# One expert's second weight matrix loaded whole, and the expert outputs joined in one piece

## The chip, the core and the metric

The kernel runs on one core of one Trainium2 chip. The metric is the time of one execution on the device in microseconds (us); for the kernel before, the median of three runs is 180.59 us (180.25 to 180.80). A profile of one execution, taken by the hardware profiler, goes with it. Its times count from the start of its span.

The engines are named as in the profile: PE multiplies matrices (PEld is its loading of weights), DVE and ACT work on vectors, POOL here does nothing but issue transfers, SP issues one. Transfers (DMA) are carried out by sixteen DMA engines.

## The reference

Attention over 8 batches of 8 heads with 576 positions and 64 columns a head, with a sliding window (four heads) or a dilated window (four heads), gives `x` of 4608 rows and 512 columns. A soft mixture of 8 experts, with 4 slots each, follows:

```python
logits = x @ phi                                  # 4608 x 32
d = softmax of logits over the rows
slot_input = d.T @ x                              # 32 x 512: 8 experts x 4 slots
for e in range(8):
    h = np.maximum(slot_input[e] @ w1[e], 0.0)    # w1[e]: 512 x 1024
    slot_out[e] = h @ w2[e]                       # w2[e]: 1024 x 512
c = softmax of logits over the 32 slots
return c @ slot_out                               # 4608 x 512, fp32
```

`w1` and `w2` of an expert have 2 MB each in fp32. They are turned to fp16 on their way into the core's memory, where each takes 1 MB.

## The kernel before, in words

**The main part** (lines 447 to 552) goes through the eight batches in a software pipeline whose order is written out by hand (`ORDER`, `STEPS`). It loads q, k and v of a batch, computes attention, the exponentials of the logits (`ET`, kept for all batches) and adds each batch's share to `U`, the sum that `slot_input` is made of. All inputs, w1 and w2 are loaded by transfers that POOL issues (`load_raw`, `load_w1`, `load_w2`), in one order for the whole kernel. POOL's transfers take turns on eight semaphores, so each issue waits until the transfer eight places ahead of it has landed.

**The order of the weights.** w1 of all experts and w2 of experts 0 to 2 are loaded between and behind the inputs. Once the last batch has left the raw buffers, line 538 gives their place to w2 of experts 3 to 7 and issues these loads (lines 545 to 549): experts 3 and 4 whole, one transfer of 1 MB each, then the left 256 columns of experts 5, 6 and 7, then their right 256 columns. A column half is two transfers of 256 KB (`load_w2` with `s`, line 208: four of the eight row blocks each).

**The experts** (lines 565 to 615). `rs` are the row sums of the softmax over the slots. `U` is divided by its last column into `si` (64 partitions: 32 slots of plain heads, 32 of dilated ones; 256 columns). `si` is turned over on PE in four transposes, two into each of two PSUM tiles `siT0` and `siT1`, and DVE copies the one and ACT the other into `siTm`, where each expert's slots stand in columns of their own. `hps` is the product with w1, `h_sb` its positive part, `hT` the transposed, `hTm` a copy of that (lines 593 to 615).

**The expert outputs** (`emit_so`, line 623). `so` is one PSUM tile of 128 partitions x 512 columns, to which all experts add. `emit_so(None, experts)` multiplies whole rows of w2 (512 columns), `emit_so(0, ...)` the left 256 columns, `emit_so(1, ...)` the right ones. The result lies in four partial sums on four groups of 32 partitions. They are joined in two steps, each for one half of 256 columns. `gather_so` copies `so` into `so_part` in fp16, 128 columns by DVE and 128 by ACT. `spread_so` multiplies with the constant `spread`, which adds the four groups up and puts the sum on all four (PSUM tile `rep`, 128 columns), and copies it into `so_sb`, again DVE for 128 columns and ACT for 128.

**The output** (`emit_fin`, line 654, and `emit_batch`, line 673). For 128 rows of the output, `f` is the product of `ET` with `so_sb`, and ACT and DVE in turn scale it with `rrow` into `om` (fp16). Four such blocks are a batch; POOL then issues the batch's store (line 676), whose transfer turns fp16 to fp32. `om[b]` lies where w1 of expert b was. The first six batches (`NHALF`) are stored in two halves of columns, the last two whole; the last 64 rows of each batch go out at the end from `om_l` (line 703).

**The order around the change** (lines 681 to 705). Every engine takes its instructions in the order of the program text, which is this:

```python
emit_so(None, (0, 1, 2, 3)); emit_so(None, (4,))
emit_so(0, (5,)); emit_so(0, (6,)); emit_so(0, (7,))
gather_so(0); spread_so(0)
for b in range(NHALF):
    if b in (2, 3, 5):
        emit_so(1, ({2: 5, 3: 6, 5: 7}[b],))
    if b == 5:
        gather_so(1)
    emit_batch(b, 0, DH)
spread_so(1)
for b in range(NHALF):
    emit_batch(b, DH, DMODEL)
```

So the left half of the columns is computed, joined and multiplied for six batches while the right halves of experts 5, 6 and 7 are still on their way; the right copy into `so_part` stands ahead of the sixth left batch, the right product and the copy into `so_sb` behind it.

Of the kernel before, what the change touches and what calls it, by code (L numbers as in the profile page):

```python
# [9 lines left out]
FP32 = mybir.dt.float32  # L10
FP16 = mybir.dt.float16
# [14 lines left out]
E_EXP = 8  # L26
S_PER_E = 4
N_SLOTS = 32
# [12 lines left out]
DH = DMODEL // 2  # L41
# [55 lines left out]
def kernel(  # L97
# [10 lines left out]
    nc = tc.nc  # L108
# [9 lines left out]
    ident = cst[:, o : o + 128]  # L118
    spread = cst[:, o + 128 : o + 256]
# [43 lines left out]
    ring = ctx.enter_context(tc.tile_pool(name="ring", bufs=2, space=bass.MemoryType.PSUM))  # L163
# [36 lines left out]
    def load_w2(e, s=None):  # L200
        src = moe_w2[e].rearrange("(p c) n -> p c n", p=128)
        if s is None:
            nc.gpsimd.dma_start(
                out=w2t[e].rearrange("p c n -> p (c n)"), in_=src.rearrange("p c n -> p (c n)")
            )
            return
        cols = slice(DH * s, DH * s + DH)
        for u in range(2):
            nc.gpsimd.dma_start(out=w2t[e][:, 4 * u : 4 * u + 4, cols], in_=src[:, 4 * u : 4 * u + 4, cols])  # L209
# [249 lines left out]
    for which in "QK":  # L459
        load_raw(which, 1)  # L460
    nc.gpsimd.dma_start(
        out=phi_raw.rearrange("p (u c) s -> p u (c s)", u=2),
        in_=moe_phi.rearrange("(u p c) s -> p u (c s)", u=2, c=2),
# [15 lines left out]
    def step(op, b):  # L479
        if op[0] in "ARM" and op[1:] in TILES:  # L480
            kind, i = TILES[op[1:]]
            if op[0] == "A":
                tmp[(op[1:], b)] = emit_av(b, kind, i)
            elif op[0] == "R":
                tmp[("R" + op[1:], b)] = emit_recip(b, kind, i, tmp[(op[1:], b)])
            else:
                engine = nc.scalar if op[1:] in ON_ACT else nc.vector
                norm_mult(b, kind, i, tmp.pop((op[1:], b)), tmp.pop(("R" + op[1:], b)), engine)
        elif op in ("S0", "S1", "S2"):
            tmp[(op, b)] = emit_scores(b, int(op[1]))  # L490
        elif op in ("E0", "E1", "E2"):
            emit_exp(b, int(op[1]), tmp.pop(("S" + op[1], b)))
        elif op in ("MK0", "MK1", "MK2"):
            emit_mask(b, int(op[2]))
        elif op[0:2] in ("QT", "KT", "VT"):
            turn(op[0], b, int(op[2]))
        elif op in ("XP0", "XP1"):
            tmp[(op, b)] = xT_plain(b, int(op[2]))
        elif op in ("XD0", "XD1"):
            tmp[(op, b)] = xT_dil(b, int(op[2]))  # L500
        elif op in ("XPc0", "XPc1", "XDc0", "XDc1"):
            xT_copy(b, op[1], int(op[3]), tmp.pop((op[0:2] + op[3], b)))
        elif op in ("VA", "VB", "VC", "VD"):
            tmp[(op, b)] = v_rows(b, "ABCD".index(op[1]))
        elif op in ("VAc", "VBc", "VCc", "VDc"):
            v_place(b, "ABCD".index(op[1]), tmp.pop((op[0:2], b)))
        elif op in ("LG", "EP"):
            tmp[(op, b)] = (back_logits if op == "LG" else back_erow)(b)
        elif op == "ET":
            back_et(b, tmp.pop(("LG", b)))  # L510
        elif op == "ER":
            back_er(b, tmp.pop(("EP", b)))
        else:
            {"ED": back_erd, "U": back_u, "UT": back_add}[op](b)

    def loads(which, b):
        load_raw(which, b)
        if which == "V":
            if b > 2:
                load_weights(1)  # L520
            if b == B - 1:
                load_weights(len(weights))
# [6 lines left out]
    for it in range(B + max(s for _, s in STEPS)):  # L529
        for op, stage in STEPS:  # L530
            b = it - stage
            if not 0 <= b < B:
                continue
            step(op, b)
            if op in frees and b + 2 < B:
                loads(frees[op], b + 2)
            left.discard((op, b))
            if w2b_pool is None and not left:
                raw_pool.release()
                w2b_pool = tc.alloc_tile_pool(name="w2b", bufs=1, side="right")  # L540
                for e in (3, 4, 5):
                    w2t[e] = w2b_pool.tile([128, 8, DMODEL], FP16, name=f"w2_{e}", tag=f"w2_{e}")
                slab_weights(6, "qk0", QK_SLAB)
                slab_weights(7, "qk1", QK_SLAB)
                for e in (3, 4):
                    load_w2(e)
                for s in range(2):
                    for e in (5, 6, 7):
                        load_w2(e, s)
        if it == 0:  # L550
            nc.vector.tensor_copy(
                out=phi4, in_=phi_raw[:, :, None, :].broadcast_to([128, 4, 4, N_SLOTS])
            )
# [21 lines left out]
        )  # L575
    nc.vector.reciprocal(out=rcol, in_=U[:, 4 * D : 4 * D + 1])
    nc.vector.tensor_scalar(out=si, in0=U[:, 0 : 4 * D], scalar1=rcol, scalar2=None, op0=ALU.mult)
    for k, copy in enumerate((nc.vector.tensor_copy, nc.scalar.copy)):
        siT = ring.tile([128, 2, N_SLOTS], FP16, name=f"siT{k}", tag="ring")
        rows = slice(32 * k, 32 * k + 32)  # L580
        for c in range(2):
            nc.tensor.transpose(siT[:, c, :], si[rows, 128 * c : 128 * c + 128], ident[rows, rows])
        diag = bass.AP(
            siTm.tensor,
            siTm.offset + 2 * k * E_EXP * N_SLOTS,
            [siTm.ap[0], (E_EXP * N_SLOTS, 2), (N_SLOTS + S_PER_E, E_EXP), (1, S_PER_E)],
        )
        copy(out=diag, in_=siT.rearrange("p c (e s) -> p c e s", e=E_EXP))
    nc.vector.reciprocal(out=rrow, in_=rs)
    hps = psum_e.tile([128, 2, 512], FP32, name="hps", tag="hps")  # L590
    h_sb = h_pool.tile([128, FDIM], FP16, name="h_sb", tag="h_sb")
# [1 line left out]
    for fc in range(2):  # L593
        for g in range(2):
            for dc in range(4):
                for j in range(4):
                    e = 4 * g + j
# [4 lines left out]
                        start=(g == 0 and dc == 0),  # L602
                        stop=(g == 1 and dc == 3),
# [3 lines left out]
    for c in range(8):  # L607
# [3 lines left out]
        out=hTm[:, 0].rearrange("p c (j s) -> p c j s", j=4)[:, :, :, 0:16], in_=hT4[:, :, :, 0:16]  # L611
    )
    nc.scalar.copy(
        out=hTm[:, 1].rearrange("p c (j s) -> p c j s", j=4)[:, :, :, 16:32], in_=hT4[:, :, :, 16:32]
# [6 lines left out]
    so = psum_so.tile([128, DMODEL], FP32, name="so", tag="so")  # L621

    def emit_so(s, experts):
        cols = slice(0, DMODEL) if s is None else slice(DH * s, DH * s + DH)
        for c in range(8):
            for e in experts:
                g, j = divmod(e, 4)
                row = 32 * (j if len(experts) == 4 else c % 4)
                nc.tensor.matmul(
                    so[row : row + 32, cols],  # L630
                    hTm[:, g, c, 32 * j : 32 * j + 32],
                    w2t[e][:, c, cols],
                    start=(e < 4 and c == 0),
                    stop=(e == 7 and c > 3),
                    skip_group_check=True,
                )

    def part_cols(s):
        c0 = DH * s
        return (nc.vector.tensor_copy, c0), (nc.scalar.copy, c0 + DH // 2)  # L640

    def gather_so(s):
        for copy, c0 in part_cols(s):
            copy(out=so_part[:, c0 : c0 + DH // 2], in_=so[:, c0 : c0 + DH // 2])

    def spread_so(s):
        for copy, c0 in part_cols(s):
            rep = ring.tile([128, DH // 2], FP32, name=f"rep_{c0}", tag="ring")
            nc.tensor.matmul(rep, spread, so_part[:, c0 : c0 + DH // 2], start=True, stop=True)
            copy(out=so_sb[:, c0 : c0 + DH // 2], in_=rep)  # L650

    turn = [0]

# [26 lines left out]

    NHALF = 6
    emit_so(None, (0, 1, 2, 3))
    emit_so(None, (4,))
    for e in (5, 6, 7):
        emit_so(0, (e,))
    gather_so(0)
    spread_so(0)
    for b in range(NHALF):
        if b in (2, 3, 5):
            emit_so(1, ({2: 5, 3: 6, 5: 7}[b],))  # L690
        if b == 5:
            gather_so(1)
        emit_batch(b, 0, DH)
    spread_so(1)
    for b in range(NHALF):
        emit_batch(b, DH, DMODEL)
    for b in range(NHALF, B):
# [4 lines left out]
    for e in range(2):  # L702
        nc.gpsimd.dma_start(
            out=rest[:, e, 512:576, :].rearrange("n i d -> i n d"), in_=om_l[64 * e : 64 * e + 64]
# [37 lines left out]
```

## Time and profile before

| | us |
|---|---|
| median of three runs | 180.59 (180.25 to 180.80) |
| the profiled execution's own time | 180.63 |
| its span, first to last instruction | 178.80 |
| busy PE, DVE, ACT, POOL in the span | 126.7, 126.3, 124.0, 56.2 |
| last whole w2 (expert 4) landed | 137.19 |
| last left piece landed, last right piece landed | 145.21, 153.24 |
| first f begins | 146.81 |
| first store issued, last store issued | 148.76, 167.67 |
| first store landed, last store landed | 154.60, 177.27 |

Transfers of POOL by kind, with the median time from issue to landing: whole weights 1 MB, 22.1 us; weight pieces of 256 KB, 15.8 us; half-width stores 512 KB, 6.2 us; whole-width stores 1 MB, 8.7 us. These times hold the wait in the queue behind earlier transfers, so they aren't the time that a transfer takes; that is read from the steps between landings.

A store or load counts as landed when all sixteen DMA engines have added their increment to its semaphore. The granted clock of PE is 0.853 in the mean, and 0.50 from 146.6 us to the end.

A row of the timeline reads: start, duration, engine, line, operation, output <- inputs, form and how many; in brackets the idle time of the engine just before, and what ended it. A row of the chain that ended last: start, duration, and what the chain stood on.

### The profile page before, as it was taken

What the parts mean: (1) busy time and instruction counts of PE and PEld (TensorE: products, weight loads), DVE (VectorE), ACT (ScalarE), POOL (GpSimd) and SP (SyncE); (2) the same over time, 40 slices, a digit from 0 to 9 for tenths busy, and PEclk for the clock granted to TensorE, in tenths of its full rate; (3) what the DMA queues carried; (4) which work ended last, traced back from release to release, by engine and by line L of the source; (5) the groups of instructions that cost most, each with busy time, mean ns of one, the idle gap of its engine ahead of it and who ended that gap; (6) DMA issues with size and microseconds to landing.
All of it is one profiled execution on the core that took longest, in us unless ns stands there. A gap on an engine that the chain in (4) does not pass through costs nothing.

```text
span 178.8 us, 4810 instructions
## 1 busy us (share of the span) xinstructions
PE 126.7 (71%) x2016; PEld 81.9 (46%) x2016; DVE 126.3 (71%) x277; ACT 124.0 (69%) x268; POOL 56.2 (31%) x94
## 2 busy tenths in 40 slices
PE   0015938988899998888988988986686856688000
PEld 0014625776666676567667657665332422221000
DVE  6464899999999999999999898275211016789200
ACT  6006758999999999999999989996301116688000
POOL 7544244224224224225420005111111515375400
PEclk9999999999999879999999699699957685555555
DMA  5999999999999999999999999999999999999994
GB/s 98 195 208 211 211 213 211 212 213 215 215 213 213 213 213 214 213 211 218 210 213 214 214 215 221 215 218 218 209 211 194 196 197 234 390 321 393 406 413 125
DMA packets 21445, 40.85 MB, mean 229 GB/s; under 512 B 1712, under 2 KB 14128, under 8 KB 20784
## 3 DMA queue, kind: packets, MB, share of 16 engines
q0 software_dynamic: 21280, 40.41, 114.3%
q8 instruction: 16, 0.26, 0.5%
q1 hardware_dynamic: 144, 0.14, 0.3%
q14 instruction: 5, 0.04, 0.1%
HBM read 62.07 MB, written 9.44 MB: 400 GB/s over the span
## 4 chain that ended last, share of the span: by engine, by line
DMA 56%; DVE 25%; PE 5%; issue 4%; ACT 3%; POOL 1%; POOLq 0%; DVEq 0%
DMA w<-in_moe_w_dram 36%; DMA rawK<-in_k_dram 9%; DVE qk L220 8%; DMA rawV<-in_v_dram 5%; DMA phi_raw<-in_moe_phi_dram 5%; DVE vT L220 5%; DVE p L282 5%; PE f L656 3%; ACT om L665 2%; DVE xd L330 2%; DVE om_l L669 1%; DVE xp L330 1%; POOL rawQ L189 1%; PE s L262 1%; DVE rc_P L317 1%
## 5 line engine op out<-in xcount | busy, mean ns | idle before, releaser
L271 ACT ACTIVATE p<-s 128x1920 f16<-128x1920 f32 (+1 forms) x24 | 42.7, 1779 | 10.9 <-PE s L262 10.8
L262 PE MATMUL s<-qk 32*128 32x128 f16 (+2 forms) x704 | 26.7, 295 | 17.9 <-DVE qk L220 12.6
L305 PEld LDWEIGHTS <-p 128*128 128x128 f16 (+1 forms) x480 | 23.0, 105 | 14.7 <-DVE xp L330 5.2
L242 ACT COPY vX<-rv 128x768 f16<-128x768 f16 (+1 forms) x32 | 25.9, 866 | 1.7 <-PE rv L236 1.7
L262 PEld LDWEIGHTS <-qk 32*128 32x128 f16 x704 | 17.2, 117 | 21.1 <-DVE qk L220 12.6
L326 ACT ACTIVATE xp<-o_P,rc_P 128x64 f16<-128x64 f32 x96 | 24.3, 406 | 2.7 <-DVE rc_P L317 2.7
L282 DVE TENSOR_TENSOR p<-p,masks 128x1920 f16<-128x1920 f16 (+1 forms) x24 | 25.4, 1083 | 0.0
L236 PE MATMUL rv<-cst,vT 128*128 128x128 f16 x176 | 18.7, 252 | 3.5 <-DVE vT L220 1.8
L220 DVE STREAM_TRANSPOSE qk<-rawQ 128x576 uint32<-128x576 uint32 x16 | 18.8, 1242 | 2.7 <-DMA rawQ<-in_q_dram 2.7
L305 PE MATMUL o_P<-vX,p 128*128 128x65 f16 (+1 forms) x288 | 20.0, 205 | 0.8 <-DVE xd L330 0.2
L220 DVE STREAM_TRANSPOSE qk<-rawK 128x576 uint32<-128x576 uint32 x16 | 19.5, 1231 | 1.1 <-DMA rawK<-in_k_dram 1.1
L220 DVE STREAM_TRANSPOSE vT<-rawV 128x576 uint32<-128x576 uint32 x16 | 19.5, 1226 | 0.7 <-DMA rawV<-in_v_dram 0.4
L236 PEld LDWEIGHTS <-vT 128*128 128x128 f16 x176 | 13.8, 128 | 8.2 <-issue 3.7
L209 POOL DMA_DIRECT2D w<-in_moe_w_dram x12 | 8.9, 746 | 26.7 <-DMA w<-in_moe_w_dram 18.7
L669 DVE TENSOR_SCALAR om<-f,rrow 128x256 f16<-128x256 f32 (+1 forms) x28 | 13.5, 519 | 4.1 <-PE f L656 3.4
L189 POOL DMA_DIRECT2D rawQ<-in_q_dram x16 | 8.9, 560 | 21.0 <-DVE rc_P L317 16.0
L665 ACT ACTIVATE om<-f,rrow 128x256 f16<-128x256 f32 (+1 forms) x28 | 12.8, 502 | 3.5 <-PE f L656 2.8
L656 PE MATMUL f<-so_sb,ET 32*128 32x256 f16 (+1 forms) x60 | 12.1, 420 | 3.7 <-ACT om L665 2.5
L676 POOL DMA_DIRECT2D out_dram<-om x14 | 10.4, 745 | 12.4 <-DVE om L669 9.4
L189 POOL DMA_DIRECT2D rawK<-in_k_dram x16 | 8.8, 551 | 17.4 <-DVE rc_P L317 15.0
L305 PE MATMUL o_D<-vX,p 128*128 128x65 f16 x128 | 10.1, 206 | 3.3 <-DVE xp L330 2.8
L189 POOL DMA_DIRECT2D rawV<-in_v_dram x16 | 8.7, 548 | 11.3 <-DVE rc_P L317 8.5
(83 smaller groups left out, 194.3 us busy)
## 6 DMA issues: line engine op xcount, KB each, us to landing
w<-in_moe_w_dram POOLq DMA_DIRECT2D x13, 1024.0 KB, 22.1
out_dram<-om POOLq DMA_DIRECT2D x12, 512.0 KB, 6.2
rawQ<-in_q_dram POOLq DMA_DIRECT2D x16, 288.0 KB, 10.8
rawK<-in_k_dram POOLq DMA_DIRECT2D x16, 288.0 KB, 10.1
rawV<-in_v_dram POOLq DMA_DIRECT2D x16, 288.0 KB, 9.8
w<-in_moe_w_dram POOLq DMA_DIRECT2D x12, 256.0 KB, 15.8
out_dram<-om POOLq DMA_DIRECT2D x2, 1024.0 KB, 8.7
out_dram<-om_l POOLq DMA_DIRECT2D x2, 512.0 KB, 9.3
```

Of the source, the lines that this page charges most:

```text
L189: nc.gpsimd.dma_start(out=t[g::2, :], in_=src[4 * g : 4 * g + 4].rearrange("h (p j) d -> (h p) (j d)", j=PJ),)
L220: nc.vector.transpose(out=out_, in_=in_)
L236: nc.tensor.transpose(rg[:, n_t, :, c, :], rows, ident)
L242: copy(out=vX[b % 2][:, t0 : t0 + n, :, 0:D], in_=rg.rearrange("p n h c d -> p n h (c d)"))
L262: nc.tensor.matmul(sps[:, h, c0 : c0 + w], kk, qq, start=(tt == 0), stop=(tt == 1))
L271: return nc.scalar.activation(out=pt, in_=sps[:, :, 0:n], func=AF.Exp, scale=SCALE)
L282: return nc.vector.tensor_tensor(out=pt, in0=pt, in1=m, op=ALU.mult)
L305: nc.tensor.matmul(o[rows, h, :], lhs, rhs, start=(n == 0), stop=(n == len(jobs) - 1), skip_group_check=True,)
L326: nc.scalar.activation(out=dst[:, h], in_=src[:, h], func=AF.Copy, scale=rc[:, h : h + 1])
L656: nc.tensor.matmul(fp[:, 0 : c1 - c0], ET[32 * j : 32 * j + 32, m : m + 128], so_sb[32 * j : 32 * j + 32, c0:c1], start=True, stop=True,)
L665: nc.scalar.activation(out=dst, in_=fp[:, 0 : c1 - c0], func=AF.Copy, scale=rrow[:, blk : blk + 1])
L669: nc.vector.tensor_scalar(out=dst, in0=fp[:, 0 : c1 - c0], scalar1=rrow[:, blk : blk + 1], scalar2=None, op0=ALU.mult)
```

## The change

w2 of expert 5 is loaded whole, behind experts 3 and 4; only experts 6 and 7 are loaded in column halves. Expert 5 is multiplied over all 512 columns ahead of the left halves, so nothing of it stands between the output batches any more. `gather_so` and `spread_so` become `join_so`: one copy of 256 columns by DVE, one product of 256 columns, one copy by ACT. The right join as a whole stands ahead of the sixth left batch. And `si` is turned over in two transposes of all 64 partitions into one PSUM tile, from which DVE and ACT copy their parts.

```diff
-                for e in (3, 4):
+                for e in (3, 4, 5):
                     load_w2(e)
                 for s in range(2):
-                    for e in (5, 6, 7):
+                    for e in (6, 7):
                         load_w2(e, s)
...
+    siT = ring.tile([128, 2, 2, N_SLOTS], FP16, name="siT", tag="ring")
+    for c in range(2):
+        nc.tensor.transpose(
+            siT[:, c].rearrange("p k s -> p (k s)"), si[:, 128 * c : 128 * c + 128], ident[0:64, 0:64]
+        )
     for k, copy in enumerate((nc.vector.tensor_copy, nc.scalar.copy)):
-        siT = ring.tile([128, 2, N_SLOTS], FP16, name=f"siT{k}", tag="ring")
-        rows = slice(32 * k, 32 * k + 32)
-        for c in range(2):
-            nc.tensor.transpose(siT[:, c, :], si[rows, 128 * c : 128 * c + 128], ident[rows, rows])
...
-        copy(out=diag, in_=siT.rearrange("p c (e s) -> p c e s", e=E_EXP))
+        copy(out=diag, in_=siT[:, :, k, :].rearrange("p c (e s) -> p c e s", e=E_EXP))
...
-    def gather_so(s):
-        for copy, c0 in part_cols(s):
-            copy(out=so_part[:, c0 : c0 + DH // 2], in_=so[:, c0 : c0 + DH // 2])
-
-    def spread_so(s):
-        for copy, c0 in part_cols(s):
-            rep = ring.tile([128, DH // 2], FP32, name=f"rep_{c0}", tag="ring")
-            nc.tensor.matmul(rep, spread, so_part[:, c0 : c0 + DH // 2], start=True, stop=True)
-            copy(out=so_sb[:, c0 : c0 + DH // 2], in_=rep)
+    def join_so(s):
+        cols = slice(DH * s, DH * s + DH)
+        nc.vector.tensor_copy(out=so_part[:, cols], in_=so[:, cols])
+        rep = ring.tile([128, DH], FP32, name=f"rep_{s}", tag="ring")
+        nc.tensor.matmul(rep, spread, so_part[:, cols], start=True, stop=True)
+        nc.scalar.copy(out=so_sb[:, cols], in_=rep)
...
-    emit_so(None, (4,))
-    for e in (5, 6, 7):
+    for e in (4, 5):
+        emit_so(None, (e,))
+    for e in (6, 7):
         emit_so(0, (e,))
-    gather_so(0)
-    spread_so(0)
+    join_so(0)
     for b in range(NHALF):
-        if b in (2, 3, 5):
-            emit_so(1, ({2: 5, 3: 6, 5: 7}[b],))
+        if b in (3, 5):
+            emit_so(1, ({3: 6, 5: 7}[b],))
         if b == 5:
-            gather_so(1)
+            join_so(1)
         emit_batch(b, 0, DH)
-    spread_so(1)
```

More of the change, by code (lines that the diff above doesn't have):

```diff
@@ L636, in emit_so @@
                 )
-    def part_cols(s):
-        c0 = DH * s
-        return (nc.vector.tensor_copy, c0), (nc.scalar.copy, c0 + DH // 2)
-    def gather_so(s):
-        for copy, c0 in part_cols(s):
-            copy(out=so_part[:, c0 : c0 + DH // 2], in_=so[:, c0 : c0 + DH // 2])
-    def spread_so(s):
-        for copy, c0 in part_cols(s):
-            rep = ring.tile([128, DH // 2], FP32, name=f"rep_{c0}", tag="ring")
-            nc.tensor.matmul(rep, spread, so_part[:, c0 : c0 + DH // 2], start=True, stop=True)
-            copy(out=so_sb[:, c0 : c0 + DH // 2], in_=rep)
+    def join_so(s):
[4 more added lines that the diff above has]
+        nc.scalar.copy(out=so_sb[:, cols], in_=rep)
     turn = [0]
```

## The prediction

> **What bounds the kernel now.** I read the page's stages first. Its rows of the DMA show no slice in which the transfers rest, and over the last eight slices the rate is that of the stores:
>
> ```profile
> DMA  5999999999999999999999999999999999999994
> GB/s 98 195 208 211 211 213 211 212 213 215 215 213 213 213 213 214 213 211 218 210 213 214 214 215 221 215 218 218 209 211 194 196 197 234 390 321 393 406 413 125
> ```
>
> The reader is to see three things: about 213 GB/s while raw inputs and weights come in (counted in fp16, so twice that is read), 194 to 197 in slices 31 to 33, where weights come in column halves, and 321 between 390 and 393 in slice 36: a hole among the stores. The chain that ended last, in order of time, then says which transfers set the pace:
>
> ```profile
> 88.33 29.17 DMA w<-in_moe_w_dram
> ...
> 117.78 24.77 DMA w<-in_moe_w_dram
> ...
> 142.83 10.41 DMA w<-in_moe_w_dram
> 153.24 0.04 issue
> 153.28 0.43 PE so L629 x4
> ```
>
> From 88.33 on it is weights until 153.24. Behind that the chain follows the matmuls of the output, but the last store is issued at 167.67 and lands at 177.27, ten us later: the transfers, not the engines, end last there too. So the end is the sum of what passes through one queue (all of it is issued by POOL), plus every time in which the queue runs dry.
>
> Durations of transfers come from the landings (issue time plus time to landing). Whole w2 pieces of 1 MB land at 112.55, 117.50, 122.34, 127.20, 132.34 and 137.19: 4.93 us each. Quarter-size pieces (256 KB, half the columns) land from 138.53 to 153.24, eleven steps of 1.338 us. Half-width stores land 1.31 us apart.
>
> The sixteen increments of one landing do not come together: those of the last weight piece stand between 150.03 and 153.24, so some of the sixteen DMA engines run 3.2 us ahead of the slowest. The hole shows that a late store costs nothing as long as it is only late for the fast ones. This is the rate from 144 to 159.3 us, 0.38 us a number:
>
> ```profile
> GB/s 181 189 199 190 200 191 199 194 196 199 193 200 193 197 195 178 260 277 303 307 324 336 375 404 399 404 361 410 402 394 412 394 410 308 254 198 174 174 353 399
> ```
>
> It falls to 174, because the sixth store is issued at 157.28 although its last om ended at 155.14; yet the last increments of stores five and six stand at 159.90 and 161.24, 1.34 apart: the slowest engine never waited. Behind the hole the increments of one store lie within 0.96 us, no longer 2.8.
>
> A second thing stands among the stores. Their last increments go 162.60, 163.86, 165.78, 167.06: one step of 1.92 for 1.31, 0.6 us more. In that stretch there is one packet that isn't ours:
>
> ```profile
> q8 instruction: 1, 0.02, 2.6%
> ```
>
> It is 16 KB of instructions, it starts at 163.19, and one engine is 1.35 us later from there on (its increments go from the midst of the others to 0.6 behind the last).
>
> **The change part by part.** All times stand against the profiled execution: span 178.80, its time 180.63, so 1.83 lie around the span; the median of the runs shown is 180.59.
>
> Weights. Four 256 KB pieces (4 x 1.338 = 5.35) become one of 1 MB (4.93). Gain 0.42: the last weight lands at 152.82. POOL issues nine instead of twelve; issues wait for the landing eight places earlier, and eight stay in flight, so no gap opens.
>
> Left half of the experts' outputs. It needed the sixth small piece, landed at 145.21. Now w2 of expert 5 lands whole first (137.19 + 4.93 = 142.12), then four left pieces: 147.47, so 2.26 later. Expert 5's eight 512-wide matmuls fill time in which PE waits for data anyway (it waits 0.92 before 145.26).
>
> Left join. These rows are the present one:
>
> ```profile
> 145.26 0.29 PE L629 MATMUL so<-w,hTm 128*32 128x256 f16 x4 [0.92 <-DMA w<-in_moe_w_dram]
> ...
> 145.60 0.29 DVE L644 CAST so_part<-so 128x128 f16<-128x128 f32 x1 [5.84 <-PE so L629]
> 145.92 0.27 ACT L644 CAST so_part<-so 128x128 f16<-128x128 f32 x1 [5.54 <-DVE so_part L644]
> 145.94 0.51 PE L649 MATMUL rep<-so_part,cst 128*128 128x128 f16 x2 [0.39 <-DVE so_part L644]
> ...
> 146.19 0.29 DVE L650 CAST so_sb<-rep 128x128 f16<-128x128 f32 x1 [0.31 <-PE rep L649]
> 146.49 0.27 ACT L650 CAST so_sb<-rep 128x128 f16<-128x128 f32 x1 [0.30 <-PE rep L649]
> ...
> 146.81 0.40 PE L656 MATMUL f<-so_sb,ET 32*128 32x256 f16 x4 [0.35 <-ACT so_sb L650]
> ```
>
> The reader is to see that ACT's first copy waits for DVE's: the two halves go one behind the other already, and 1.21 us pass from 145.60 to 146.81. A 256-wide copy isn't in the trace. Below it lies the 128-wide one (0.29 on DVE, 0.27 on ACT), above it the 256-wide om (0.48, 0.47), which also multiplies. DVE's om grows by 0.27 from 256 to 512 columns, so 0.13 for 128: 0.42 on DVE, 0.37 on ACT, nearer the upper rows. The product is 0.22 (a 128-wide rep) to 0.40 (256-wide f at granted clock 0.50): 0.38. With 0.04 at each hand-over: 0.42 + 0.04 + 0.38 + 0.04 + 0.37 + 0.05 = 1.30; the ends are 0.9 and 1.5. Ahead of it the four matmuls take 0.41 and not 0.29, since the clock is 0.50 from 146.6 on. So f starts at 147.47 + 0.05 + 0.41 + 0.05 + 1.30 = 149.28. From f to the last om of the first batch are 1.40 (146.81 to 148.21), to POOL's issue 0.55 more (148.76): the first store is issued at 151.23, 2.5 later than now.
>
> What is late next. The fast engines have by then been idle since about 149.6 - 0.4, the slowest ends its weights at about 152.5. A store into idle engines lands 3.0 (first increment) to 3.2 us (tenth) after its issue, by the sixth store of the present trace: 154.4. An uninterrupted queue would give 152.82 + 1.34 = 154.16. Now it is 154.60. Of the gain of 0.42, 0.2 remain, and all sixteen engines are in step from here.
>
> The instruction block. From the first store to the end are now 177.27 - 154.60 = 22.67, 0.6 of it the block: 22.07 without. With engines in step nobody is far enough behind to hide it, and it costs its 1.35. PE has 12 of its 2016 matmuls fewer (8 in emit_so, 2 transposes, 2 rep), each with its weight load; the block now comes when 5 matmuls are left. I take it that it still comes, as it goes by PE's place in its program: 154.45 + 22.07 + 1.35 = 177.87, which is 0.6 later than 177.27.
>
> Right join. Om of the first three batches ends at 150.68, 151.60, 152.52 (0.92 a batch); the fourth stands behind eight matmuls of expert 6 (1.30, as the third now): 153.82, the fifth 154.74. On PE the join's rep waits for DVE's copy, which is queued behind the fifth batch's om, and the sixth batch's f wait behind rep; ACT's copy stands ahead of its om. That is 0.05 + 1.30 to f and 0.85 to two om: 156.95, issue at 157.5. The queue needs it by 157.8 (the fifth store lands at 159.69, its data 0.4 earlier, a new issue needs 1.2 to reach the engines). So it costs 0, with 0.3 to spare. Right stores follow 0.95 apart against 1.31 a transfer, and gain.
>
> siT in one tile: two transposes instead of four, in a stretch (130.0 to 130.8) hidden by weights that land until 147.47: 0. Uncovered it would be some 0.2.
>
> Sum: 180.63 + 0.6 = 181.2.
>
> [...]
>
> **Rivals.** A: the block costs nothing among the stores, since PE's program ends before it is fetched, or since it falls on an engine that waits. For: only 5 matmuls are left behind it now, and 12 go. [...] Then the end is 154.45 + 22.07 = 176.5, 0.75 sooner: 179.9.
>
> B is the forecast, 181.2.
>
> C, slower: the sixth store is late again. Now it goes out 2.1 us after its last om (155.14 to 157.28), though the semaphores it waits for had come; what held it I don't know. If the hold belongs to this place, behind the right join, it is issued at 159.05, not 157.5, and with engines in step the queue runs dry from 157.8: 1.2 us. It decides as soon as the issue is later than 157.8. Time 182.4 with the block (181.1 without). Against it: three issues fewer ahead may move it to where stores are early.
>
> That the change doesn't do what it says: two serial copies become one, so the join hardly shortens (1.21 against 1.30); this is in the sum.
>
> **How the numbers follow.** This kernel's measurement tells about 0.3% (0.54 us) from no change: faster is below 180.05, slower above 181.13. A 0.27 (179.6 to 180.3, two thirds of it faster); B 0.48 (180.8 to 181.7, for the join's ends, over half slower); C 0.25, nearly all slower. So 0.18 faster, 0.30 same, 0.52 slower. Range 179.8 to 182.4, from most of A to C.
>
> **What would show it.** First store issued at 151.2 and a dip of the rate ahead of it, with the increments of its landing close together; last weight at 152.8; sixth store at 157.5 and no second hole; a 16 KB packet of queue 8 after 163 and one landing step of about 2.7 (absent in A). It is wrong if the first store goes out before 150.9, or after 151.8.

## The result

The changed kernel takes 181.38 us (median of nine runs, 180.87 to 181.90), the kernel before 180.44 us in the same nine rounds. The ratio is 1.0046, its 95% interval 1.0032 to 1.0059: slower by half a per cent. The forecast was 181.2 us, with 179.8 to 182.4 as range. The time came out close to it by luck: as shown below, the step that was to bring it did not happen, and another one did.

The profiled execution of the changed kernel is the fastest of its nine: 180.87 us, span 178.8 (the median of the nine spans is 179.3). So its rows show where the time goes, and not the whole of the difference: the spans of the two profiled executions are the same (178.8). Of the 0.94 us between the medians, some 0.6 lie within the span (179.3 against 178.7 in the median) and about a quarter of a us outside it.

The page's stages, changed kernel:

```profile
DMA  5999999999999999999999999999999999999997
GB/s 105 193 210 208 213 213 212 211 213 215 212 214 214 212 214 215 213 211 215 213 213 217 212 216 220 214 220 214 211 220 214 189 197 144 403 344 324 408 410 220
```

There are three low slices where one was: 144 (slice 34), 344 (36) and 324 (37). Two narrower views show them, the rate from 144 to 159.3 us and from 156 to 171 us, 0.38 us a number:

```profile
GB/s 182 193 198 189 203 191 197 194 198 198 192 201 194 191 145 127 123 104 90 59 158 408 412 388 407 407 415 386 412 407 388 402 404 396 383 404 402 303 8 238
```

```profile
GB/s 412 399 380 402 401 399 213 3 330 401 421 380 415 401 407 393 412 401 380 410 407 391 44 0 246 404 415 391 404 407 412 393 401 410 399 431 421 410 421 404
```

The first hole (145 down to 59) is the one forecast: the fast DMA engines have finished their weights and wait for the first store (the increments of the last weight stand from 149.60 to 152.51). It doesn't reach 0, since the slowest engines still work. The other two, at about 158.6 and 164.5, go to 3 and 0: there all sixteen wait, and no packet of data runs from 158.74 to 159.04 and from 164.45 to 165.12. In the kernel before, the one hole went to 174 and no further.

POOL's issues say which stores those are (start, duration; in brackets the wait before it):

```profile
155.53 0.75 POOL L670 DMA_DIRECT2D out_dram<-om  x1 [0.68 <-DVE so_part L641]
157.73 0.75 POOL L670 DMA_DIRECT2D out_dram<-om  x1 [1.45 <-ACT om L659]
158.67 0.75 POOL L670 DMA_DIRECT2D out_dram<-om  x1 [0.20 <-ACT om L659]
159.61 0.75 POOL L670 DMA_DIRECT2D out_dram<-om  x1 [0.20 <-ACT om L659]
161.01 0.75 POOL L670 DMA_DIRECT2D out_dram<-om  x1 [0.65 <-ACT om L659]
163.79 2.96 POOL L670 DMA_DIRECT2D out_dram<-om  x4 [2.04 <-DVE om L663]
```

157.73 is the sixth store, behind the right join. 163.79 is the tenth (the fourth right one), with three more at its heels: its last om ended at 161.45, an issue comes 0.53 to 0.56 later where POOL isn't still busy with the ones ahead, and this one comes 2.3 later. The row names DVE's om as what ended the wait; but that had long been done.

The landings (last of sixteen increments, in us) put prices on it:

| | before | after |
|---|---|---|
| last weight | 153.24 | 152.51 |
| first store issued, landed | 148.76, 154.60 | 150.55, 154.04 |
| increments of the first store lie within | 2.8 | 0.5 |
| step to the 6th store | 1.34 | 1.89 |
| step to the 9th store (the block before) | 1.92 | 1.21 |
| step to the 10th store | 1.28 | 2.21 |
| last store landed | 177.27 | 177.42 |

Against 1.31 a step, the sixth store brings 0.58 and the tenth 0.90. The first store lands 0.56 earlier, the step of the block is 0.6 less, and the other steps together 0.17 less: +0.15, the difference of the last row.

The left join, to set beside the rows of before:

```profile
147.16 0.29 PE L630 MATMUL so<-w,hTm 128*32 128x256 f16 x4 [1.02 <-DMA w<-in_moe_w_dram]
...
147.50 0.42 DVE L641 CAST so_part<-so 128x256 f16<-128x256 f32 x1 [8.00 <-PE so L630]
147.97 0.27 PE L643 MATMUL rep<-so_part,cst 128*128 128x256 f16 x1 [0.52 <-DVE so_part L641]
...
148.28 0.37 ACT L644 CAST so_sb<-rep 128x256 f16<-128x256 f32 x1 [8.16 <-PE rep L643]
148.70 0.29 PE L650 MATMUL f<-so_sb,ET 32*128 32x256 f16 x4 [0.46 <-ACT so_sb L644]
```

From the copy to f are 1.20 us, against 1.21 in two halves: the join in one piece costs no time of its own here, and gains none.

Two more rows of the page matter for all that follows, the packets of queue 0 (all of POOL's transfers) and the 16 KB blocks of instructions on queue 8. Before:

```profile
q0 software_dynamic: 21280, 40.41, 114.3%
q8 instruction: 16, 0.26, 0.5%
```

After:

```profile
q0 software_dynamic: 19312, 40.41, 112.7%
q8 instruction: 15, 0.25, 0.5%
```

The bytes are the same. 21280 packets are 1330 for each of the sixteen DMA engines, 19312 are 1207. And one block of instructions fewer is fetched.

### The profile page after: what moved, and what is told of

The parts are those of the page before. It is cut to its first block, busy times and chain, and to the rows that moved or that the text cites. A ratio compares the mean times of both kernels' runs of the same rounds, so it can differ in the third digit from the quotient of the medians.

```text
span 178.8 us, 4778 instructions
## 1 busy us (share of the span) xinstructions
PE 123.7 (69%) x2004; PEld 79.9 (45%) x2004; DVE 126.4 (71%) x275; ACT 123.5 (69%) x266; POOL 53.7 (30%) x91
## 3 DMA queue, kind: packets, MB, share of 16 engines
q0 software_dynamic: 19312, 40.41, 112.7%
## 4 chain that ended last, share of the span: by engine, by line
DMA 47%; ACT 23%; DVE 11%; PE 8%; issue 4%; POOL 1%; POOLq 0%; DVEq 0%; ACTq 0%
DMA w<-in_moe_w_dram 32%; DMA rawK<-in_k_dram 10%; ACT p L271 6%; DMA phi_raw<-in_moe_phi_dram 5%; PE f L650 4%; ACT vX L242 4%; DVE qk L220 4%; ACT xp L326 4%; ACT om L659 4%; DVE p L282 2%; ACT xT L365 2%; ACT xT L367 2%; ACT xd L326 1%; DVE vT L220 1%; PE rv L236 1%
## 5 line engine op out<-in xcount | busy, mean ns | idle before, releaser
L271 ACT ACTIVATE p<-s 128x1920 f16<-128x1920 f32 (+1 forms) x24 | 45.7, 1904 | 11.1 <-PE s L262 11.0
L242 ACT COPY vX<-rv 128x768 f16<-128x768 f16 (+1 forms) x32 | 28.9, 990 | 1.7 <-PE rv L236 1.7
L326 ACT ACTIVATE xp<-o_P,rc_P 128x64 f16<-128x64 f32 x96 | 27.9, 553 | 2.0 <-DVE rc_P L317 2.0
L262 PEld LDWEIGHTS <-qk 32*128 32x128 f16 x704 | 17.7, 117 | 23.0 <-DVE qk L220 12.8
L305 PEld LDWEIGHTS <-p 128*128 128x128 f16 (+1 forms) x480 | 22.0, 101 | 11.7 <-issue 3.7
L236 PE MATMUL rv<-cst,vT 128*128 128x128 f16 x176 | 17.5, 243 | 3.3 <-DVE vT L220 1.8
L236 PEld LDWEIGHTS <-vT 128*128 128x128 f16 x176 | 13.3, 124 | 7.3 <-issue 3.8
L650 PE MATMUL f<-so_sb,ET 32*128 32x256 f16 (+1 forms) x60 | 13.4, 410 | 3.7 <-ACT om L659 2.8
L209 POOL DMA_DIRECT2D w<-in_moe_w_dram x8 | 6.0, 745 | 29.4 <-DMA w<-in_moe_w_dram 25.0
L365 ACT COPY xT<-rp 128x576 f16<-128x576 f16 x16 | 12.0, 965 | 1.4 <-PE rp L346 1.4
```

The lines of the kernel that those rows point to most:

```text
L236: nc.tensor.transpose(rg[:, n_t, :, c, :], rows, ident)
L242: copy(out=vX[b % 2][:, t0 : t0 + n, :, 0:D], in_=rg.rearrange("p n h c d -> p n h (c d)"))
L262: nc.tensor.matmul(sps[:, h, c0 : c0 + w], kk, qq, start=(tt == 0), stop=(tt == 1))
L271: return nc.scalar.activation(out=pt, in_=sps[:, :, 0:n], func=AF.Exp, scale=SCALE)
L305: nc.tensor.matmul(o[rows, h, :], lhs, rhs, start=(n == 0), stop=(n == len(jobs) - 1), skip_group_check=True,)
L326: nc.scalar.activation(out=dst[:, h], in_=src[:, h], func=AF.Copy, scale=rc[:, h : h + 1])
```

## The experiments

**Theory.** A transfer's packets per engine can be counted from its rows and the sizes of packets in the trace: a 256 KB piece or a half-width store has 33 (512 rows over 16 engines, and one of 4 bytes for the semaphore; before has 1440 of these, 16 for each of POOL's 90 transfers), a whole w2 has 9 (packets of 8192 bytes), a w1 has 17 (4096), a raw load 5 (4608). Over all transfers these add up to the 1330 and 1207 of the page. Before, 999 lay ahead of the sixth store, and it ended at 1032. After, 711 lie ahead of the first store; nine stores make it 1008, and the tenth ends at 1041. The packets 1009 to 1032 are in both. So I took it that POOL holds the one issue with which queue 0 passes a count in this range, which I put at about 1024 as an estimate, for 1.6 us before (issue 2.1 behind the last om) and 1.8 after, and that this hold, moved from a place where it was covered to one where it is not, is what the change costs. Rivals: the hold belongs to the place behind the right join, or to a time; or the joins cost, or the holes add up in another way.

### The loading alone

```diff
 kernel before
-                for e in (3, 4):
+                for e in (3, 4, 5):
...
-                    for e in (5, 6, 7):
+                    for e in (6, 7):
...
-        if b in (2, 3, 5):
-            emit_so(1, ({2: 5, 3: 6, 5: 7}[b],))
+        if b in (3, 5):
+            emit_so(1, ({3: 6, 5: 7}[b],))
```

> The kernel before, with only w2 of expert 5 loaded whole (joins and siT as before). My theory is that POOL holds the one store with which queue 0 passes 1024 packets per DMA engine: 1330 packets per engine before, 999 of them ahead of the 6th store, so the 6th is held; 711 ahead of the first store after, so the 10th is. This kernel has the same packets as the changed one, so the 10th store (4th right one) is held by some 1.8 us and the 6th goes out without a hold, within 0.6 us of its last om. The right half is ready about 0.5 us earlier than in the changed kernel, so the end comes 0.3 to 0.6 us earlier than there: 180.8 to 181.1 us. Rival: the hold belongs to the place behind the right copy and falls on the 6th store again; then there is a hole at the 6th and none at the 10th.

Measured: 181.24 us, ratio 1.0032 (1.0019 to 1.0046). POOL's issues around the tenth store:

```profile
160.92 0.74 POOL L676 DMA_DIRECT2D out_dram<-om  x1 [0.68 <-ACT om L665]
163.69 2.96 POOL L676 DMA_DIRECT2D out_dram<-om  x4 [2.03 <-DVE om L669]
```

The hold is on the tenth, and the sixth (156.85) lands in its turn, 1.37 behind the fifth. The joins are those of before, so neither they nor the place behind them make the hold. The time is 0.1 to 0.4 longer than I had expected.

### The joins alone

```diff
 changed kernel
-                for e in (3, 4, 5):
+                for e in (3, 4):
...
-                    for e in (6, 7):
+                    for e in (5, 6, 7):
...
-    for e in (4, 5):
-        emit_so(None, (e,))
-    for e in (6, 7):
+    emit_so(None, (4,))
+    for e in (5, 6, 7):
         emit_so(0, (e,))
...
-        if b in (3, 5):
-            emit_so(1, ({3: 6, 5: 7}[b],))
+        if b in (2, 3, 5):
+            emit_so(1, ({2: 5, 3: 6, 5: 7}[b],))
```

> The changed kernel, but w2 of expert 5 in column halves as before (so joins, siT and the place of the right join alone are changed). Packets as before, so by my theory the hold is on the 6th store, which now has its om later by the right join (about 157.0 where 155.14 was): issue about 159, the queue is dry before it by over 1 us even for the slowest engine. Time 181.3 to 181.9 us. Rival (the loading alone costs the time, the joins are free): as before, 180.4 to 180.7 us.

Measured: 181.59 us, ratio 1.0062 (1.0050 to 1.0075). The hold is on the sixth store again, as with all kernels that have 1330 packets an engine:

```profile
153.87 0.74 POOL L670 DMA_DIRECT2D out_dram<-om  x1 [0.20 <-issue]
158.25 5.16 POOL L670 DMA_DIRECT2D out_dram<-om  x7 [3.64 <-DVE om L663]
```

It waits for the right join first and is held behind it, 158.25 where 157.28 was. The queue runs dry for all engines, so these are in step (the increments of the sixth store lie within 0.23 us), and the block of instructions, which comes here too (at 164.24), costs 1.31 at one step (2.62) where it had cost 0.6. The time is in the range that I had expected, but not for the reason given: the step to the held store is 1.53, so the slowest engine lost 0.2 there and not over 1 us; most of the rest is what the block cost more than before.

### The right join behind the sixth left batch

```diff
 changed kernel
-        if b == 5:
-            join_so(1)
         emit_batch(b, 0, DH)
+    join_so(1)
```

> The changed kernel with the whole right join moved behind the sixth left batch. By my theory the end hangs on the issue of the 10th store, the held one, and that follows from when the right half is joined and multiplied: the hole ahead of the 6th store (landing step 1.89 for 1.31) goes, the one ahead of the 10th (2.21) grows by about as much, and the time stays within 0.3 us of the changed kernel's 181.38. Rival: the two holes add up, and the time falls by 0.6 us to 180.8.

Measured: 181.88 us, ratio 1.0085 (1.0065 to 1.0106), 0.5 us slower than the changed kernel: neither number was right. POOL's issue of the tenth store:

```profile
164.71 1.49 POOL L670 DMA_DIRECT2D out_dram<-om  x2 [2.04 <-DVE om L663]
```

The hole ahead of the sixth store (step 1.26 now) isn't gone but stands ahead of the seventh, which waits for the join (step 2.31). The right half comes later, the tenth store is issued at 164.71 and not at 163.79, 0.92 later, and the last store lands 0.95 later. That agrees with an end that hangs on the held store. Whether the two holes add up, this run doesn't tell, since the first hole was moved and not removed. The run of the loading alone says more: there the sixth store lands in its turn, the tenth is held all the same, and the last store lands at 177.32, within 0.1 of the changed kernel's. I had overlooked that the later join puts off the held store's om.

### Twelve transposes more

```diff
 changed kernel
-    for c in range(8):
+    for c in (*range(8), *range(4), *range(8)):
         nc.tensor.transpose(hT[:, c, :], h_sb...[:, c, :], ident)
```

> The changed kernel with twelve transposes of h_sb done twice (they write the same values), so that PE has as many matmuls and weight loads as before the change. They take about 1.1 us ahead of 139.6, in a stretch that waits for weights. My theory: the 16 KB block of instructions that came at 163.19 before and doesn't come in the changed kernel comes again near the end, and since the sixteen DMA engines are in step, one landing step is 2.5 or so for 1.31 and the time is 1.0 to 1.35 us longer, about 182.5 us. Rival: no 16th block, or one that costs nothing: 181.4 us.

Measured: 182.16 us, ratio 1.0088 (1.0072 to 1.0103). The block is back. This is the rate from 163 to 168 us, 0.125 us a number, and the queue's row in that stretch:

```profile
GB/s 393 426 336 393 418 401 418 393 393 401 418 393 377 271 0 0 0 0 0 0 270 385 401 385 393 377 393 369 410 418 336 402 410 426 393 410 418 393 426 393
...
q8 instruction: 1, 0.02, 1.3%
```

The packet comes at 164.70, just ahead of the hole before the tenth store, and the step to that store is 2.98 where 2.21 was: 0.77. That is less than the 1.0 to 1.35 expected, since part of it falls into the hole. So the number of PE's instructions decides whether this block comes among the stores: with 2016 and 2012 matmuls it came at 163 to 165, with 2008 behind the last store in two profiles (180.56 and 180.75) and not at all in a third, with 2004 not at all within the profile.

### The hold moved into the weights

```diff
 changed kernel
-        src = moe_w2[e].rearrange("(p c) n -> p c n", p=128)
+        src = moe_w2[e].rearrange("(c p) n -> p c n", p=128)
...
-                out=w2t[e].rearrange("p c n -> p (c n)"), in_=src.rearrange("p c n -> p (c n)")
+                out=w2t[e], in_=src
...
-        ... h_sb.rearrange("p (q l) -> p l q", l=8)[:, c, :]
+        ... h_sb.rearrange("p (l q) -> p l q", l=8)[:, c, :]
```

> The changed kernel with another spread of w2's rows over partitions (row c*128+p at place c of partition p, where 8p+c was; h is turned over to match, the result is the same). A whole w2 then has 65 packets per DMA engine instead of 9, so 1047 come ahead of the first store, and by my theory the hold falls on the last weight piece, where it is covered by 10 us of queue. The hole ahead of the 10th store goes (0.9 us); the one ahead of the 6th stays. Against it stands the rate of the smaller packets: six whole w2 at 4.93 us each become 0 to 8% slower, 0 to 2.4 us. So I expect no hold among the stores, and a time of 180.5 to 182.5 us; measured from the landing of the last weight to the end it should be 0.7 to 1.0 us shorter than in the changed kernel. Rival (place or time decides, not the packets): the 10th store is held as in the changed kernel.

Measured: 182.20 us, ratio 1.0091 (1.0069 to 1.0113). POOL's issue of the last weight piece and of the ninth to eleventh store:

```profile
138.33 0.74 POOL L209 DMA_DIRECT2D w<-in_moe_w_dram  x1 [4.30 <-DMA w<-in_moe_w_dram]
144.92 0.75 POOL L209 DMA_DIRECT2D w<-in_moe_w_dram  x1 [5.85 <-DMA w<-in_moe_w_dram]
```

```profile
162.64 0.74 POOL L670 DMA_DIRECT2D out_dram<-om  x1 [0.66 <-ACT om L659]
163.60 0.74 POOL L670 DMA_DIRECT2D out_dram<-om  x1 [0.22 <-ACT om L659]
164.57 0.74 POOL L670 DMA_DIRECT2D out_dram<-om  x1 [0.22 <-ACT om L659]
```

The last weight piece is held for 1.6 us (its wait of 5.85 against 4.30), and no store is: the tenth goes out 0.96 behind the ninth. From the first store's landing to the last are 22.65 us, against 23.38. The whole w2 became 0.1 to 0.2 us slower each, the last weight landed 1.26 later, and that is more than the gain. From the last weight's landing to that of the last store it is 0.42 shorter, less than I had expected, because the first store is issued 0.4 later against it.

### The hold moved by one store

```diff
 changed kernel
+        if s is None and e in (3, 4, 5):
+            for u in range(2):
+                nc.gpsimd.dma_start(out=w2t[e][:, 4 * u : 4 * u + 4, :], in_=src[:, 4 * u : 4 * u + 4, :])
+            return
```

> The changed kernel with the whole w2 of experts 3, 4 and 5 loaded as two transfers each (row blocks 0 to 3 and 4 to 7). That adds 9 packets per DMA engine for each, 27 in all: 738 ahead of the first store. By my theory the hold moves by one store, from the 10th to the 9th. The 9th then lands about 1.2 us later than in the changed kernel and the rest follow in a closed queue; the time is 0.1 to 0.4 us longer, 181.5 to 181.8 us. Rival (place in the program or time decides): the 10th store is held, 181.4 us.

Measured: 181.89 us, ratio 1.0078 (1.0059 to 1.0097).

```profile
160.09 0.75 POOL L674 DMA_DIRECT2D out_dram<-om  x1 [0.20 <-ACT om L663]
163.34 3.69 POOL L674 DMA_DIRECT2D out_dram<-om  x5 [2.51 <-ACT om L663]
```

Now the ninth store is held (160.09 is the eighth, five follow in a row). 27 packets moved it by one store, to the place that the count says. It costs 0.1 more than I had expected.

### The stores issued by SP

```diff
 changed kernel, and the kernel before
-    om = [w1_pool.tile([128, 4, DMODEL], FP16, ...
-    om_l = h_pool.tile([128, B // 2, DMODEL], FP16, ...
+    om = [w1_pool.tile([128, 4, DMODEL], FP32, ...
+    om_l = h_pool.tile([128, B // 2, DMODEL], FP32, ...
...
-        nc.gpsimd.dma_start(       # the stores
+        nc.sync.dma_start(
```

> The changed kernel with om kept in fp32 and all stores issued by SP instead of POOL, so that no store goes through queue 0. By my theory there is no hold among the stores, so the end comes at least 0.9 us earlier: 180.0 to 180.5 us if the stores' rate stays at 1.31 us a half-width store. Rival: writing 4-byte om slows ACT and DVE or the transfers, and the time is the same or longer than 181.4 us.

> The kernel before with om in fp32 and the stores issued by SP. There the hold cost the slowest DMA engine nothing, so by my theory little is gained: the hole ahead of the 6th store goes, the block of instructions stays, and the time is within 0.3 us of 180.5 (or lower by as much as the issue by SP is faster at the first store, which is not the bound). Rival: the hold did cost time, through all engines that waited: 179.5 us or less.

Measured: 184.15 us (ratio 1.0200, 1.0180 to 1.0220) and 181.64 us (1.0057, 1.0040 to 1.0075). Both forecasts were wrong. There is no hold among the stores, but a half-width store steps by 1.52 us in the first and 1.36 in the second, where POOL's took 1.31, and the two stores of om_l by 2.1 to 2.4 and 1.9 to 2.0, where they took 1.25. So these two agree with the count, since queue 0 stays at 711 and 834 packets an engine here, and say nothing on the price of the hold. Whether SP has such a hold they don't tell either: its queue comes to 505.

### The hold moved to the twelfth store

```diff
 changed kernel, and the one with the loading alone
-            out=w1t[e].rearrange("p (u c) f -> p u (c f)", u=2),
-            in_=moe_w1[e].rearrange("(u p c) f -> p u (c f)", u=2, p=128),
+            out=w1t[e].rearrange("p k f -> p (k f)"),
+            in_=moe_w1[e].rearrange("(p k) f -> p (k f)", p=128),
```

> The changed kernel with w1's rows dealt to partitions in one block of four (row 4p+k) and not as two of two, so that a w1 transfer has 9 packets per DMA engine instead of 17; the bytes are the same. The rows no longer match those of the slots' inputs, so this kernel's product with w1 is another one than the reference's. 647 packets come ahead of the first store, so by my theory the hold moves from the 10th to the 12th store (6th right one), where the queue is longer: the hole of 0.9 us ahead of the 10th goes, up to 0.5 us may come ahead of the 12th. Time 0.4 to 0.9 us below the changed kernel's 181.38: 180.5 to 181.0 us. Rival (the held store isn't what sets the end): no gain, 181.2 to 181.6 us.

> The kernel before with w2 of expert 5 whole (joins as before), and w1's rows dealt as blocks of four (its product with w1 is another one than the reference's; same bytes). Hold on the 12th store instead of the 10th. My theory: the loading alone would have been a small gain but for where the hold falls; 0.5 to 0.8 us below the 181.24 of the same kernel with the hold on the 10th store, so 180.4 to 180.8 us. Rival: 181.2 us.

Measured: 180.37 us (ratio 0.9991, 0.9974 to 1.0008) and 180.12 us (0.9984, 0.9963 to 1.0005). The first one's issues and its rate from 156 to 171 us:

```profile
162.86 0.74 POOL L670 DMA_DIRECT2D out_dram<-om  x1 [0.22 <-ACT om L659]
165.69 2.22 POOL L670 DMA_DIRECT2D out_dram<-om  x3 [2.08 <-ACT om L659]
```

```profile
GB/s 407 396 380 404 407 396 104 25 396 412 412 385 407 412 388 410 404 407 382 410 401 371 410 404 399 377 410 401 352 240 412 410 393 426 431 421 421 410 426 388
```

The held store is the twelfth, and where the rate fell to 0 it now dips to 240 once: the queue is long enough there (104 and 25 are the hole ahead of the sixth). With the same bytes and the same joins the time is 1.0 us lower than the changed kernel's, and with the loading alone 1.1 us lower (0.9 by the two ratios). So the hold on the tenth store is the price of the change; without it, it would be no slower than before. How much of the 1.0 us is the hold alone is less sure. From the first store's landing to the last, the two profiles are 0.56 and 0.66 us shorter (22.82 against 23.38, 22.70 against 23.36). The rest lies outside that stretch. A faster loading of w1 doesn't show as its cause: the last weight lands at 152.06 and 153.22, where it was 152.51 and 152.22, earlier in the one and later in the other. Both gain a little more than I had expected.

### PE's instructions, in the kernel before

```diff
 kernel before
             for dc in range(4):
+                if fc == 0 and (dc == 2 or (dc == 1 and g == 1)):
+                    continue
                 for j in range(4):
```

> The kernel before, with twelve of the 64 products with w1 left out (so part of the sum over w1's rows is missing in the first half of h). They stand in a stretch that waits for weights. PE then has as many instructions as in the changed kernel. My theory: the last 16 KB block of instructions, which came at 163.19 and cost 0.6 us at the step from 163.86 to 165.78, doesn't come among the stores, the hold stays on the 6th store and costs nothing, and the time is 0.4 to 0.6 us lower: 179.9 to 180.2 us. Rival: the block comes all the same, or another engine takes its place as the last: 180.5 us.

Measured: 180.00 us, ratio 0.9972 (0.9957 to 0.9987). As expected, the block is gone from the stores, the step from the eighth store to the ninth is 1.34 and not 1.92, the sixth store is held as before (issued at 157.13), and the last store lands at 176.57 instead of 177.27. The queue's row of this run, to set beside the 16 of before:

```profile
q8 instruction: 15, 0.25, 0.5%
```

### Three stores by SP

```diff
 the kernel with the loading alone
+    om32 = {}   # for b in range(3): in the place of w1_b, left half fp32, right half fp16
...
+        src = om32[b][c0 // DH] if b in om32 else om[b][:, :, c0:c1]
...
+        queue = nc.sync if b in om32 and c0 == 0 else nc.gpsimd
+        queue.dma_start(
```

> The kernel before with w2 of expert 5 whole, and the first three left stores written as fp32 and issued by SP. Queue 0 then passes 1024 packets with the 13th store (the 7th batch), where the queue is longest, and the result is the reference's. A store issued by SP took 1.5 us where one by POOL took 1.31, so three of them cost up to 0.6 us; the hole ahead of the 10th (1.1 us) goes, up to 0.4 us may come ahead of the 13th. Time 180.4 to 181.0 us. It beats the kernel before (180.5) only if SP's stores lose less than that. Rival: the two queues disturb each other and it is slower than 181.2 us.

Measured: 180.24 us in the median, ratio 1.0001 (0.9979 to 1.0023): no difference from the kernel before. The hold went where the count says, to the thirteenth store (its issue at 167.16 comes 3.36 behind the twelfth), and there its step is 3.35 where 2.6 is usual for a batch stored whole. So this version, 0.2 us faster than I had expected, takes back what the change cost and doesn't beat the kernel before.

## Why the prediction was right, and where it was wrong

- **What bounds the kernel** held: the queue of transfers, from the weights to the last store. What the profiles show of each version's time is when the weights and the stores landed; a part outside the span comes to it (see there).
- **The weights** held: a whole w2 at 4.9 us, the last weight 0.73 earlier (0.42 forecast). The first of the six landings listed there as w2, 112.55, is that of the last w1; the step is right all the same.
- **The left join** held in kind and was sized 0.7 us too late: first store at 150.55, forecast 151.23. The last left piece landed at 147.12 and not at 147.47, and PE's granted clock was not yet at 0.50 (1.00 up to 149.0), so the four matmuls took 0.29 and rep 0.27. The 256-wide copies took 0.42 and 0.37, just as worked out.
- **All engines in step** held: the increments of the first store lie within 0.5 us. From there on a late issue shows at its landing step: 0.58 at the sixth store and 0.90 at the tenth, where the hold of before left the step at 1.34.
- **The instruction block failed.** The step read "I take it that it still comes". It doesn't: 15 blocks, not 16. That was rival A's condition, and it is right that the number of PE's instructions decides (twelve transposes bring it back, twelve products fewer remove it from the kernel before). Its price in the sum, 1.35 with all engines in step, was sound: with the joins alone, where they are in step and the queue is full, it cost 1.31 at one step. It cost 0.5 to 0.8 us of time in the two that change PE's instructions alone, where the late engine had been ahead of the slowest, or part of it fell into a hole. What failed is that the block comes at all; its 1.35 had no place in the sum.
- **The right join** was sized wrong at the point of need. It read "The queue needs it by 157.8". A store into an empty queue lands 3.3 us after its issue (3.31 the sixth, 3.33 the tenth), an uninterrupted one 1.31 after the one ahead: 159.14 + 1.31 - 3.3 = 157.15. Issued at 157.73 it cost 0.58, not 0. The forecast's own terms, 159.69 - 0.4 - 1.2, give 158.1 and not 157.8; the fifth store landed 0.55 earlier than forecast. The issue, 0.2 later than forecast, hides two errors: the first store went out 0.68 earlier, and from there to the sixth it took 7.18 us for 6.27, since the third and fifth batch took 1.34 and 1.43 and not 0.92. But this hole did not move the end, which hung on the tenth store: with the loading alone, which lacks this hole, the last store lands at 177.32 and here at 177.42.
- **Rival C** had the mechanism that paid, a hold of POOL's issue that no semaphore explains, and I had called its cause unknown. I placed it behind the right join, and against it I wrote that fewer issues "may move it to where stores are early". It moved, by the 123 packets that the change saves, to a store that was not early enough. It cost 0.90 at its step; where it fell elsewhere, the stretch of the stores was 0.56 to 0.73 us shorter, and with the same bytes the median was 1.0 lower.
- **Outside the span** lies a difference that I had not allowed for: 2.06 to 2.19 us in all kernels with the new join and siT, 1.8 to 1.9 mostly in those with the old. It is about a quarter of a us of the 0.94. Neither the loading nor the number of matmuls sets it (the kernel with twelve transposes more has 2.15, that with twelve products fewer 1.83); which of the edits does, was not tried and stays open.
- **The signs** that the forecast named speak against it. It called itself wrong if the first store went out before 150.9, and that store went out at 150.55. The 16 KB block and the step of 2.7 are absent, and there is a second hole.

So the forecast of 181.2 was right by its sign and its size, and that was luck: the block that was missing (1.35 in the sum) was made up for by the hold that had moved and by the part outside the span, which the sum left out. Its chance for slower, 0.52, rested on a reason that it only half had.

## What to carry to other kernels

When the queue of transfers sets the end, ask of a change not only how many bytes it moves but how many packets, and look in the trace for what the queue does as the count grows. Here one hold of POOL cost nothing at its landing step before (1.34 for 1.31), where the slowest of the sixteen engines ran 2.8 us behind the fastest, and 0.90 us after (2.21), where they were in step within 0.5 us and waited together. And a term that isn't work of the kernel (a block of instructions, a wait that no semaphore explains) is worth counting in the trace first: here the packets and blocks on the page's third part, compared between two kernels, led to both.

## What was not expected of the hardware

**POOL held one issue where its queue passes 1015 to 1032 packets per DMA engine.** All fourteen profiles, before and after among them, agree: the held transfer is the 6th store (999 packets ahead, 1032 behind it), the 9th (1002, 1035), the 10th of POOL's stores (1008, 1041), the 12th (1010, 1043), the last weight piece (1014, 1047), and nothing where queue 0 passes 711 or 834 in all. What the five have in common are the packets 1015 to 1032; the 1024 of the expectations is an estimate in this range, and no run shows the count closer. The hold is 1.6 to 1.9 us long. What POOL does in it, no run shows; nor how it goes on beyond 1543 packets, the most that any run has.

**A block of 16 KB of instructions among the stores cost 0.5 to 0.8 us of time** in the two runs that change PE's instructions alone, and 1.31 us at one landing step where all engines were in step. In the trace it is one packet of 16384 bytes on queue 8, which the profile calls instruction; in the kernel before it started at 163.19 and took 1.04 us. The last of the sixteen increments alone comes late by it (with the joins alone 1.58 us behind the first, where 0.28 was). Twelve matmuls more or fewer in PE's program, 2016 or 2004, decided whether it came; by what mechanism, no run shows.

**Stores of fp32 by SP were slower than stores by POOL that turn fp16 into fp32**: 1.36 to 1.52 us a half-width store against 1.31. The issue itself came sooner by SP, 0.09 us behind the last om of the first store against 0.56. So for these stores (512 rows of 1 KB) the way of SP was faster at the issue and slower at the landings. The type of om differs as well as the engine that issues, so which of the two makes the landings slower is not shown.
